# Two layouts of PSUM and the output product among the filler, in a two-layer attention and GLU kernel

## The chip, the cores and the metric

The kernel runs on one core of a Trainium2 chip. The metric is the device time of one execution in microseconds (us). Engines are named as in the profile: PE (matmul), PEld (its weight loads), DVE, ACT, POOL, and SP, whose queue issues most DMAs. PSUM, where PE writes its products, has eight banks of 128 x 512 numbers in fp32 here; DVE and ACT read it.

## The reference

Two layers; each is attention with 16 heads that share one key and one value head, then a gated linear unit. S = 2048 tokens, D = 448, 16 heads of 28, F = 1792.

```python
def _A_ref(x, wq, wk, wv, wo):
    q = (x @ wq).reshape(B, S, H, Dh).transpose(0, 2, 1, 3)
    k = x @ wk
    v = x @ wv
    scores = jnp.einsum("bhqd,bkd->bhqk", q, k) * (Dh ** -0.5)
    o = jnp.einsum("bhqk,bkd->bhqd", _softmax(scores), v)
    return o.transpose(0, 2, 1, 3).reshape(B, S, H * Dh) @ wo
def _B_ref(x, w_gate, w_up, w_down):
    return (_sigmoid(x @ w_gate) * (x @ w_up)) @ w_down
x = x + _A_ref(_layernorm(x), wq, wk, wv, wo)
x = x + _B_ref(_layernorm(x), w_gate, w_up, w_down)
x = x + _A_ref(_layernorm(x), wq, wk, wv, wo)
x = x + _B_ref(_layernorm(x), w_gate, w_up, w_down)
```

## The kernel before

The program is written out instruction by instruction: on each engine, instructions run in the order in which the Python code issues them. What sets that order is a hand-made interleaving of three kinds of work.

**Attention steps.** A layer has 16 query tiles u of 128 rows and, for each, 16 key tiles kt of 128 keys, so 256 steps. One step makes four score tiles s (`scores`, L485, one for each group of four heads; PE product, then an exp on ACT into P, L491), multiplies the four P of the step before with the values into pv (`pv`, L494), and makes the row maxima of four heads of the next query tile against 512 keys (`mx_gen`, L442: four PE products mx into four banks, four reductions on DVE, L462). The string ORDER sets the order within a step: S is one score tile, P is pv, M the maxima, X runs the side work that is due, F hands a slice of time to the filler. Before, it is FSFSFSFSPXM. In query tile 0, two steps (kt 5 and 10, MORE) run M twice. After the 16 groups of one query tile, the maxima are reduced further (m32, m16), transposed on PE (mt), copied (mr) and stored by a DMA from POOL's queue into row 28 of the query tile QS, so that the scores come out with the maximum already taken off.

**Side stages** of a finished query tile (`Block.tile`, L535): sums, reciprocals, oT, the output product wo (`fc`, L584), layer norm, transposition into XT2. Each stage has a delay in steps; `tick` (L514), at X, runs those that are due. `fc` issues its 12 matmuls at once.

**Filler** (`Filler`, L727): generators that issue one matmul at a time, as many as a slice of time pays for: the GLU of a block of two query tiles (`bulk`: gp, up, dn) and the query projections qp of the coming blocks (`qgen`). The rate is the work left over the steps left, until step 48 for the first, and 32 steps for each block. A block's GLU can begin when both of its query tiles are through all side stages, at step 48 at the earliest (`fed`).

In layer 0, `paced` (L269) also runs the preparation of the weights at X: sums of squares on ACT (rmax, L109), then scaling and splitting (sgu, L129, on ACT; L130 on DVE; L140 to L142 on POOL).

Between the layers a loop (L921) ticks, gives four slices of filler each time, and every fifth time (every time for the last four) issues one group of layer 1's maxima for query tile 0, once the keys of those 512 are there (`mx_ready`). The keys come from the GLU's output: dn, layer norm, transposition, kv, transposition into KK.

One PSUM bank is pv's (`psv`). The other seven are one pool, tag f, from which s, mx, qp, gp, up, dn, wo, kv and mt each take a bank that is free:

```python
    NBK = {"f": 7, "s": 2, "m": 3}
    psf = ctx.enter_context(tc.tile_pool(name="psf", bufs=1, space=PSUM))
```

A bank stays taken from the first matmul of a product until its last reader is done; for a product of the filler that is over several steps.

Of the kernel before, what the change touches and what calls it, by code (L numbers as in the profile page):

```python
# [8 lines left out]
F32 = mybir.dt.float32  # L9
# [10 lines left out]
def interleaved_layers_kernel(ctx: ExitStack, tc: tile.TileContext, x, wq, wk, wv, wo, wg, wu, wd, out, layers=2):  # L20
# [23 lines left out]
    BANKS = {"s": "f", "m": "f"}  # L44
    NBK = {"f": 7, "s": 2, "m": 3}
    psf = ctx.enter_context(tc.tile_pool(name="psf", bufs=1, space=PSUM))
# [33 lines left out]
    def fps(shape, dt, name):  # L80
        flush()
        return psf.tile(shape, dt, tag="f", name=name, bufs=NBK["f"])

# [243 lines left out]
    def chain(ps, W, X, cost, w_first):  # L327

        pairs = PAIRS if w_first else sorted(PAIRS, key=lambda a: a[2])
        for n, (part, c, xc, k) in enumerate(pairs):  # L330
            a, b = W(part, c, k), X(xc, k)
            if not w_first:
                a, b = b, a
            nc.tensor.matmul(ps, a, b, start=n == 0, stop=n == 10)  # L334
            yield cost
    sums = [drm.tile([G, 512], F32, name=f"sums{i}") for i in range(2)]
# [34 lines left out]
    def qproj(l, XT, b, g):  # L371
        p = fps([128, 512], F32, "qp")
        yield from chain(p, lambda a, c, k: WQ[:k, a, c, 4 * g:4 * g + 4].rearrange("p h d -> p (h d)"),
                         lambda c, k: XT[:k, c], C512, True)
        by_pool = early[0]
# [21 lines left out]
        defer(ev)  # L397

# [9 lines left out]
    late = []  # L408
    stored = set()
    LT = 1  # L410
# [26 lines left out]
    def mx_ready(l, n):  # L437

        u, r = divmod(n, 4 * NB)
        return KVD[l] >= 4 * (r // 4 + 1) if u == 0 else True  # L440

    def mx_gen(l):  # L442

        load_qh(l, 0)
        for u in range(U):
            qh = QH[l, u]
            mp = wk1.tile([128, 4, 4, NB], F32, name="mp", bufs=2)
            for kb in range(NB):
                for g in range(G):
                    for i in range(len(late) - 1, -1, -1):  # L450
                        late[i][0] -= 1
                        if late[i][0] <= 0:
                            late.pop(i)[1]()
                    assert KVD[l] >= 4 * (kb + 1)
                    ps = [psf.tile([128, 512], F32, tag=BANKS["m"], name="mx", bufs=NBK[BANKS["m"]])
                          for _ in range(4)]
                    for h in range(4):
                        nc.tensor.matmul(ps[h], qh[32 * h:32 * h + 32, g],  # L458
                                         KK[l][32 * h:32 * h + 32, 1, kb * 512:(kb + 1) * 512], start=True,
                                         stop=True, tile_position=(32 * h, 0))  # L460
                    for h in range(4):
                        nc.vector.tensor_reduce(mp[:, g, h, kb:kb + 1], ps[h], axis=AX.X, op=OP.max)  # L462
                    ps = None
                    if kb == NB - 1 and g == 2 and u + 1 < U:
                        load_qh(l, u + 1)
                    if kb * 4 + g == 7:
                        load_qs(l, u)
                    yield
            m32 = wk1.tile([128, 16], F32, name="m32")
            m16 = wk1.tile([128, 16], F16, name="m16")  # L470
            nc.vector.tensor_reduce(m32, mp.rearrange("p g h k -> p (g h) k"), axis=AX.X, op=OP.max)
            nc.vector.tensor_scalar(m16, m32, -(2.0 ** -15), None, op0=OP.mult)

            def fin(u=u, m16=m16):
                stored.add(("m", l, u))
                p = fps([16, 128], F16, "mt")
                nc.tensor.transpose(p, m16, id16)
                r = wk1.tile([16, 128], F16, name="mr")
                nc.vector.tensor_copy(r, p)
                nc.gpsimd.dma_start(QS[l, u][28:29].rearrange("o g h n -> o (g h) n"), r)  # L480
            late.append([LT, fin])
        while late:
            late.pop(0)[1]()
# [468 lines left out]
```

## Time and profile before

| | |
|---|---|
| median of 3 runs | 2375.84 us (2373.78 to 2376.23) |
| span of the profiled execution | 2370.5 us |
| instructions | 40937 |
| first score product of layer 0, of layer 1 | 116.49 us, 1284.04 us |
| last exp of layer 0 | about 1161 us |
| GLU work begins within layer 0, layer 1 | 292.82 us, 1447.92 us |

The page says for each engine how long it was busy. Below, rows of the timeline have the start in us, how long the row lasts, engine, line, operation, output and inputs, how many instructions were merged, and in brackets how long the engine idled before it and what ended the wait. Matmul rows of one kind overlap, so starts, not lengths, give what a matmul costs PE.

### The profile page before, as it was taken

The page shows a single profiled execution, that of the slowest core. Times are in us where ns is not written, and L with a number is a line of the kernel's source. Part 1 is how long each engine was busy: PE and PEld are TensorE (multiplying, and loading weights), DVE is VectorE, ACT ScalarE, POOL GpSimd, SP SyncE. Part 2 cuts the span into 40 slices and gives each one's busy share as a digit, 9 for nine tenths or more (in the row PEclk, how much of TensorE's full clock was granted, in tenths as well). Part 3 has the DMA queues.
Part 4 walks back from the last instruction along what each step waited for, and adds up shares of the span by engine and source line. Part 5 has one row for each costly group of instructions (what it writes and reads, how often), then busy time and mean ns, then how long its engine had stood idle before and what let it go on. Part 6 is the DMA issues. An engine that isn't in the chain of part 4 may idle for free.

```text
span 2370.5 us, 40937 instructions
## 1 busy us (share of the span) xinstructions
PE 2226.5 (94%) x15592; PEld 990.3 (42%) x15592; DVE 1624.5 (69%) x2858; ACT 1560.6 (66%) x2583; POOL 348.7 (15%) x621
## 2 busy tenths in 40 slices
PE   3688899999999999999999989999999999999999
PEld 1221244444444444444573223444444444444456
DVE  3787787777767777774258887777677776777321
ACT  5497767676667767777513777767676776777751
POOL 5403565001111010101011011000000000000010
PEclk9899999999999999999999999999999999999999
DMA  5433563322223132322342112322232222222133
GB/s 145 132 115 95 155 197 111 102 85 71 90 70 108 55 101 85 91 94 63 108 136 57 27 49 82 95 63 87 62 106 63 89 63 91 86 81 93 57 109 120
DMA packets 227525, 218.57 MB, mean 92 GB/s; under 512 B 159408, under 2 KB 187760, under 8 KB 227328
## 3 DMA queue, kind: packets, MB, share of 16 engines
q1 hardware_dynamic: 220832, 200.11, 28.3%
q0 software_dynamic: 5376, 14.87, 1.7%
q8 instruction: 122, 2.00, 0.3%
q10 hardware_dynamic: 1120, 0.98, 0.1%
q14 instruction: 75, 0.61, 0.1%
HBM read 175.37 MB, written 23.59 MB: 84 GB/s over the span
## 4 chain that ended last, share of the span: by engine, by line
PE 78%; DVE 11%; ACT 3%; DMA 2%; issue 2%; SPq 1%; POOL 0%; ACTq 0%; DVEq 0%; POOLq 0%
PE pv L499 19%; PE s L488 16%; PE dn L680 11%; PE gp L334 10%; PE up L334 10%; DVE mp L462 8%; PE mx L458 6%; PE wo L590 3%; ACT P L491 2%; PE qp L334 2%; DVE st L289 0%; DMA qd<-qst 0%; DMA sums<-rc 0%; DMA lb<-sums 0%; DMA XT<-hl 0%
## 5 line engine op out<-in xcount | busy, mean ns | idle before, releaser
L491 ACT ACTIVATE P<-s,esc 128x512 f32<-128x512 f32 x2048 | 1309.2, 690 | 513.2 <-PE s L488 496.1
L462 DVE TENSOR_REDUCE mp<-mx 128x1 f32<-128x512 f32 x2048 | 1268.2, 683 | 408.0 <-PE mx L458 404.1
L488 PE MATMUL s<-QS,KK 96*128 96x512 f16 x2048 | 761.4, 382 | 61.8 <-DVE mp L462 41.1
L334 PEld LDWEIGHTS <-wgu 128*128 128x128 f16 x4928 | 458.1, 97 | 243.5 <-issue 96.8
L499 PE MATMUL pv<-P,VV 128*32 128x512 f32 x4096 | 549.2, 609 | 0.0
L334 PE MATMUL up<-XT,wgu 128*128 128x256 f16 x2464 | 375.6, 272 | 0.0
L334 PE MATMUL gp<-XT,wgu 128*128 128x256 f16 x2464 | 374.2, 273 | 0.2
L680 PE MATMUL dn<-WD,h 128*128 128x448 f16 x1344 | 321.7, 352 | 0.0
L488 PEld LDWEIGHTS <-KK 96*128 96x128 f16 x2048 | 193.1, 97 | 181.3 <-issue 107.9
L458 PE MATMUL mx<-KK,QH 32*128 32x512 f16 x2048 | 217.8, 389 | 17.3 <-DVE mp L462 5.3
L458 PEld LDWEIGHTS <-QH 32*128 32x128 f16 x2048 | 53.6, 91 | 396.8 <-issue 385.6
L680 PEld LDWEIGHTS <-h 128*128 128x128 f16 x1344 | 124.1, 98 | 135.8 <-issue 22.0
L499 PEld LDWEIGHTS pv<-P,VV 128*32 128x32 f32 x4096 | 81.0, 108 | 206.0 <-issue 193.9
L573 POOL TENSOR_TENSOR lb<-pvs,lb 128x512 f32<-128x512 f32 x32 | 40.5, 1265 | 789.0 <-DMA lb<-sums 647.5
L654 ACT ACTIVATE h<-th 128x512 f16<-128x512 f32 x112 | 70.4, 629 | 86.0 <-DVE th L651 85.8
L295 POOL TENSOR_SCALAR rs<-mv 128x1 f32<-128x1 f32 (+2 forms) x53 | 13.4, 252 | 702.4 <-DVE mv L290 691.6
L651 DVE SCALAR_TENSOR_TENSOR th<-th,up 128x512 f32<-128x512 f32 x112 | 76.1, 679 | 56.9 <-PE up L334 44.4
L334 PE MATMUL qp<-XT,WQ 128*128 128x512 f16 x352 | 108.7, 409 | 2.5 <-DVE mp L462 1.2
L655 DVE SCALAR_TENSOR_TENSOR h<-th,h 128x512 f16<-128x512 f32 x112 | 78.8, 703 | 46.1 <-ACT h L654 46.1
L643 ACT ACTIVATE th<-gp,gsc 128x512 f32<-128x512 f32 x112 | 76.9, 687 | 45.8 <-PE gp L334 45.8
L590 PE MATMUL wo<-WO,oT 128*128 128x448 f16 x384 | 78.3, 353 | 0.2 <-DVE oT L580 0.2
L334 PEld LDWEIGHTS <-WQ 128*128 128x128 f16 x352 | 34.0, 102 | 61.3 <-issue 38.8
(117 smaller groups left out, 787.8 us busy)
## 6 DMA issues: line engine op xcount, KB each, us to landing
wgu<-wgu_d SPq DMA_DIRECT2D x224, 512.0 KB
QS<-qd SPq DMA_DIRECT2D x384, 32.0 KB
lb<-sums SPq DMA_DIRECT2D x128, 64.0 KB
xr<-in_A_x_dram SPq DMA_DIRECT2D x32, 224.0 KB
qd<-qst POOLq DMA_DIRECT2D x28, 256.0 KB, 2.6
wgu_d<-sgu POOLq DMA_DIRECT2D x14, 512.0 KB, 3.8
QH<-qd SPq DMA_DIRECT2D x28, 128.0 KB
x2d<-x SPq DMA_DIRECT2D x16, 224.0 KB
```

Source lines behind the costliest of these rows:

```text
L334: nc.tensor.matmul(ps, a, b, start=n == 0, stop=n == 10)
L458: nc.tensor.matmul(ps[h], qh[32 * h:32 * h + 32, g], KK[l][32 * h:32 * h + 32, 1, kb * 512:(kb + 1) * 512], start=True, stop=True, tile_po ...
L462: nc.vector.tensor_reduce(mp[:, g, h, kb:kb + 1], ps[h], axis=AX.X, op=OP.max)
L488: nc.tensor.matmul(s, KK[l][0:96, 0, kt * 128:(kt + 1) * 128], QS[l, u][:, g].rearrange("p h n -> p (h n)"), start=True, stop=True)
L491: nc.scalar.activation(p, s, AF.Exp, scale=esc)
L499: nc.tensor.matmul(v[32 * g:32 * g + 32], VV[l][:, kt], P[g], start=kt == 0, stop=kt == KT - 1, tile_position=(0, 32 * g))
L590: nc.tensor.matmul(p, v["oT"][:, a, h * 128:(h + 1) * 128], WO[:, c, h], start=n == 0, stop=n == 11)
L643: defer(lambda: nc.scalar.activation(th, gp.rearrange("p j n -> p (j n)"), AF.Tanh, scale=gsc))
L651: nc.vector.scalar_tensor_tensor(t, th, 1.0, up.rearrange("p j n -> p (j n)"), op0=OP.add, op1=OP.mult)
L654: nc.scalar.activation(h[:, 0], t, AF.Copy, scale=2.0 ** -17)
L655: defer(lambda: nc.vector.scalar_tensor_tensor(h[:, 1], t, 2.0 ** -17, h[:, 0], op0=OP.mult, op1=OP.subtract), 1)
L680: nc.tensor.matmul(p, hs[f // 2][:, a, o:o + 128], WD[:, f, c], start=n == 0, stop=n == 3 * FC - 1)
```

## The change

There are five parts.

- **PSUM in two layouts.** `layout(kind)` closes one pool and opens another. "even" is the seven banks of before. "split" has three banks with tag f (s, qp, wo, kv, mt and all others) and two tiles of two banks each with tag m for maxima. "split" holds from the program's start, and from each layer's start, until the first block of the layer is fed; then "even". In "split", one DVE reduction takes two heads at once from a tile of two banks.
- **Order within a step.** XSSSFPMFS in "split", XFSFSFSFSPM in "even".
- **wo among the filler.** `fc` only puts a generator on the list `urgent`; each slice issues up to three of its matmuls, ahead of other filler. The stages behind wo are scheduled when it is done.
- **Maxima.** mt follows four slices after the reduction (LAG), by way of `defer`, in place of the next M. mr's DMA is issued from SP's queue in place of POOL's. In layer 1, query tile 0 takes the last 512 keys in two halves, so that the first can run before the last two key tiles are there. The loop between the layers issues a group at every third tick in place of every fifth. QH of the next layer is loaded in the last query tile of the layer before.
- **Query projections of layer 1** for blocks 2 and 3 go to the filler between the layers, in place of layer 1's start.

```diff
-    NBK = {"f": 7, "s": 2, "m": 3}
-    psf = ctx.enter_context(tc.tile_pool(name="psf", bufs=1, space=PSUM))
+    NBK = {"even": 7, "split": 3}
+    def layout(kind):
...
+        banks["scope"] = tc.tile_pool(name=f"psf{banks['n']}", bufs=1, space=PSUM, reuse_waits="tile")
+    def bank(shape, dt, name):
+        return banks["pool"].tile(shape, dt, tag="f", name=name, bufs=NBK[banks["kind"]])
+    def four():
+        if banks["kind"] == "even":
+            ps = [bank([128, 512], F32, "mx") for _ in range(4)]
+            return [(1, p, [p]) for p in ps]
+        ps = [banks["pool"].tile([128, 2, 512], F32, tag="m", name="mx", bufs=2) for _ in range(2)]
+        return [(2, p, [p[:, 0], p[:, 1]]) for p in ps]
...
+    LAG = 4
+    KEYS = {False: [0, 512, 1024, 1536, 2048], True: [0, 512, 1024, 1536, 1792, 2048]}
...
-                    for h in range(4):
-                        nc.vector.tensor_reduce(mp[:, g, h, kb:kb + 1], ps[h], axis=AX.X, op=OP.max)
+                    for n, p, _ in ps:
+                        src = p[:, :k1 - k0] if n == 1 else p[:, :, :k1 - k0]
+                        nc.vector.tensor_reduce(mp[:, g, h:h + n, kb:kb + 1], src, axis=AX.X, op=OP.max)
...
-                nc.gpsimd.dma_start(QS[l, u][28:29].rearrange("o g h n -> o (g h) n"), r)
+            nc.sync.dma_start(QS[l, u][28:29].rearrange("o g h n -> o (g h) n"), r)
...
+            def fc():
+                fill.urgent.append(wo_gen())
...
+            n = 0
+            while self.urgent and n < 3:
+                c = self.next(self.urgent[0])
...
-    ORDER = "FSFSFSFSPXM"
+    ORDERS = {"even": "XFSFSFSFSPM", "split": "XSSSFPMFS"}
...
-        if l:
-            for b in range(2, NB):
-                fill.add(qgen(l, b), G * QCH)
         fill.slice(QCH)
+        layout("split")
...
+            if (l, 0) in BLK and BLK[l, 0].fed == TB:
+                layout("even")
```

What this makes of the order, at three places.

PE in layer 0, query tile 0, before: the four score products of one step with a filler matmul among them, and the start of pv. The names' numbers tell buffers apart; P_1307 to P_1319 are the exps of the step before. In brackets is the engine whose progress the instruction waits for.

```order
L488 MATMUL s_1340<-QS_878,KK_120 128x512 [waits Activation_49]
L334 LDWEIGHTS WQ_89
L334 MATMUL qp_1160<-XT0_127,WQ_89 128x512
L488 LDWEIGHTS KK_120
L488 MATMUL s_1345<-QS_878,KK_120 128x512 [waits DVE_49]
L488 LDWEIGHTS KK_120
L488 MATMUL s_1349<-QS_878,KK_120 128x512 [waits Activation_49]
L488 LDWEIGHTS KK_120
L488 MATMUL s_1353<-QS_878,KK_120 128x512 [waits DVE_49]
L499 MATMUL pv_1213<-P_1307,VV_121 32x512
```

The same place in the change: s_1367 is the last score product of one step, s_1374 to s_1382 are the first three of the next, and P_1344 to P_1369 the exps of the step before.

```order
L531 MATMUL s_1367<-QS_846,KK_120 128x512 [waits Activation_49]
L531 LDWEIGHTS KK_120
L531 MATMUL s_1374<-QS_846,KK_120 128x512 [waits Activation_49]
L531 LDWEIGHTS KK_120
L531 MATMUL s_1378<-QS_846,KK_120 128x512 [waits Activation_49]
L531 LDWEIGHTS KK_120
L531 MATMUL s_1382<-QS_846,KK_120 128x512 [waits Activation_49]
L357 LDWEIGHTS WQ_86
L357 MATMUL qp_1300<-XT0_127,WQ_86 128x512
L542 MATMUL pv_1140<-P_1344,VV_121 32x512
```

Before, the four waited for DVE and ACT in turn, since banks of mx and s mixed; now each waits for ACT alone. s_1374 and s_1382 lie in one bank, s_1367 and s_1378 in another, and qp_1300 is open in the third: s_1382 waits for the exp of s_1374. pv, the next mx and the fourth s stand behind it.

ACT in the same step of the change: P_1369 is the exp of s_1367, P_1376 that of s_1374; rmax is a square of the weights' preparation.

```order
L534 ACTIVATE P_1369<-s_1367,esc_97 128x512 [waits PE_49]
L132 ACTIVATE rmax_1339,mall_791<-rmax_1339 128x784 [waits DMAHW2_49,Activation_49]
L534 ACTIVATE P_1376<-s_1374,esc_97 128x512 [waits PE_49]
L534 ACTIVATE P_1380<-s_1378,esc_97 128x512 [waits PE_49]
L534 ACTIVATE P_1384<-s_1382,esc_97 128x512 [waits PE_49]
L534 ACTIVATE P_1401<-s_1399,esc_97 128x512 [waits PE_49]
```

The square stands between the exp of the last s of a step and that of the first s of the next, as X is now the first letter of a step; before, it stood ahead of the step's four exps as well, but most s waited for DVE or for an exp of the step before.

PE in layer 1, query tile 0, in the change, where no filler is left:

```order
L531 MATMUL s_15451<-QS_14618,KK_1048 128x512 [waits Activation_49]
L531 LDWEIGHTS KK_1048
L531 MATMUL s_15455<-QS_14618,KK_1048 128x512 [waits Activation_49]
L531 LDWEIGHTS KK_1048
L531 MATMUL s_15459<-QS_14618,KK_1048 128x512 [waits Activation_49]
L531 LDWEIGHTS KK_1048
L531 MATMUL s_15463<-QS_14618,KK_1048 128x512 [waits Activation_49]
L542 MATMUL pv_15438<-P_15428,VV_1049 32x512
```

Here all three banks serve s: s_15463, the third of its step, takes the bank of s_15451, the fourth of the step before. Before the change, a step here read as in the first rows, with one or two qp matmuls.

More of the change, by code (lines that the diff above doesn't have):

```diff
@@ L81, in fps @@
         flush()
-        return psf.tile(shape, dt, tag="f", name=name, bufs=NBK["f"])
+        return bank(shape, dt, name)
     C512, C448, C256, C128, C32 = 216, 190, 110, 56, 110
@@ L465, in mx_gen @@
+                    ps = p = src = b = None
+                    if k1 == S and g == 2 and u + 1 < U:
                         load_qh(l, u + 1)
@@ L738, in run, with next, finish @@
         def run(self, gen):
+            cur[0] = None
             for c in gen:
                 self.debt -= c
+        def next(self, gen):
+            cur[0] = gen
+            return next(gen, None)
+        def finish(self):
+            for gen in self.urgent + [g[0] for g in self.gens]:
+                while gen in mid:
+                    self.debt -= self.next(gen) or 0
         def slice(self, ns):
@@ L874, in interleaved_layers_kernel @@
             layer_tiles(l + 1)
-        if l:
-            for b in range(2, NB):
-                fill.add(qgen(l, b), G * QCH)
         fill.slice(QCH)
+        layout("split")
         flush(True)
         next(mx, None)
-        while late:
-            late.pop(0)[1]()
         fill.slice(QCH)
@@ L888, in interleaved_layers_kernel @@
             P = []
+            if (l, 0) in BLK and BLK[l, 0].fed == TB:
+                layout("even")
+            ORDER = ORDERS[banks["kind"]]
             for o in ORDER:
@@ L920, in interleaved_layers_kernel @@
         n = done = 0
-        while (side or pend or fill.gens) if final else (side or pend or done < 4 * NB):
+        last = G * len(parts_of(l + 1, 0))
+        while side or pend or fill.urgent or (fill.gens if final else done < last):
             tick()
```

123 lines of the change are left out of this document (82 added, 41 removed).

## The prediction

> **What bounds the kernel now.** I read first the page's busy lines, then the table by stretches, then, for the stretches where PE idles, the waits of PE and the timeline of single steps. The median of the runs is 2375.84 us; the sum below is made against the profiled execution, whose span is 2370.5 us, so 5.3 us lie around the span.
>
> ```profile
> PE 2226.5 (94%) x15592; PEld 990.3 (42%) x15592; DVE 1624.5 (69%) x2858; ACT 1560.6 (66%) x2583; POOL 348.7 (15%) x621
> 150.00:200.00 50.00, 42.43 (x244) 9.99 (x243) 41.13 (x71) 45.49 (x86) 2.52 (x3) 0.98 0.42 121
> 1300.00:1350.00 50.00, 45.30 (x262) 10.82 (x261) 42.12 (x71) 36.26 (x62) 2.00 (x3) 0.97 0.05 16
> 1500.00:1600.00 100.00, 99.31 (x711) 44.81 (x708) 71.91 (x123) 69.87 (x111) 5.27 (x11) 1.00 0.26 81
> ```
>
> The columns are the stretch in us, its length, busy us of PE, PEld, DVE, ACT and POOL, granted clock, DMA. With GLU work as filler (1500 to 1600) PE has 99% and is the bound: there only added or removed PE work, or new idle, changes the time. In the first 48 steps of each layer (150 to 200, 1300 to 1350) PE has 85 to 91%, and no engine is full. So the change is decided by the step's cycle of waits in those stretches, and by the passage between the layers. One regular step of layer 1, before:
>
> ```profile
> 1293.86 1.07 PE L499 MATMUL pv<-P,VV 128*32 128x512 f32 x8
> 1294.86 0.40 PE L458 MATMUL mx<-KK,QH 32*128 32x512 f16 x4
> 1295.18 0.60 PE L488 MATMUL s<-QS,KK 96*128 96x512 f16 x2
> 1295.28 2.48 DVE L462 TENSOR_REDUCE mp<-mx 128x1 f32<-128x512 f32 x4 [0.58 <-PE mx L458]
> 1295.61 2.42 ACT L491 ACTIVATE P<-s,esc 128x512 f32<-128x512 f32 x4 [0.37 <-PE s L488]
> 1296.62 0.38 PE L488 MATMUL s<-QS,KK 96*128 96x512 f16 x1 [0.22 <-DVE mp L462]
> 1296.93 1.06 PE L499 MATMUL pv<-P,VV 128*32 128x512 f32 x8
> ```
>
> The period is 1296.93 - 1293.86 = 3.07. The last s waits for a bank that DVE frees, pv and the next mx stand behind it, and DVE idles 0.58: a loop of PE and DVE. From these rows: pv to mx 1.00, mx to s 0.32, s to its exp 0.43, last s to pv 0.31. An exp to the s that waits for its bank takes 1379.48 - 1378.74 = 0.74, and exps follow each other at (2.42 - 0.69) / 3 = 0.58:
>
> ```profile
> 1372.43 0.69 ACT L491 ACTIVATE P<-s,esc 128x512 f32<-128x512 f32 x1 [2.63 <-PE s L488]
> 1378.74 2.42 ACT L491 ACTIVATE P<-s,esc 128x512 f32<-128x512 f32 x4 [0.60 <-PE s L488]
> 1379.48 0.82 PE L488 MATMUL s<-QS,KK 96*128 96x512 f16 x2 [0.56 <-ACT P L491]
> ```
>
> **The split layout, a new loop.** Three banks now serve s, qp, wo and mt. By the changed order a step is s1 s2 s3, filler, pv, mx, filler, s4. With all three banks on s, s3 takes the bank of the s4 before it and waits for that exp. pv and mx, ready long before, stand behind s3 on PE, and s4 behind them; ACT runs dry meanwhile. The loop is exp4 to s3 0.74, s3 to pv 0.31, pv to mx 1.00, mx to s4 0.32, s4 to exp4 0.43 to 0.47: **2.81 us**. The DVE loop no longer closes: its four maxima take 2.4, and mx needs only the tile of two heads that was reduced a step earlier.
>
> With a product open in one of the three banks, two are left: s3 waits for exp1 of its own step, which ACT starts 0.58 after exp4: 0.58 + 0.74 + 1.63 + 0.45 = **3.40**. Each filler matmul lies between s3 and s4 and adds its 0.22. Anything that ACT does between exp4 and exp1 adds its full time too. In layer 0 that is a square of the weights (124.61 to 125.45: 0.84) or an sgu copy (237.76 to 238.40: 0.64):
>
> ```profile
> 124.61 0.93 ACT L109 ACTIVATE rmax<-rmax 128x784 f32<-128x784 f32 x1
> 125.45 2.50 ACT L491 ACTIVATE P<-s,esc 128x512 f32<-128x512 f32 x4
> 237.76 0.73 ACT L129 ACTIVATE sgu<-rgu,swb 128x512 f16<-128x512 f32 x1
> 238.40 2.42 ACT L491 ACTIVATE P<-s,esc 128x512 f32<-128x512 f32 x4
> 1301.42 4.88 DVE L462 TENSOR_REDUCE mp<-mx 128x1 f32<-128x512 f32 x8 [0.58 <-PE mx L458]
> 1369.30 2.44 PE L590 MATMUL wo<-WO,oT 128*128 128x448 f16 x12
> 1371.68 0.39 PE L458 MATMUL mx<-KK,QH 32*128 32x512 f16 x4
> 119.79 1.06 PE L499 MATMUL pv<-P,VV 128*32 128x512 f32 x8
> 291.49 1.06 PE L499 MATMUL pv<-P,VV 128*32 128x512 f32 x8
> 1287.72 1.06 PE L499 MATMUL pv<-P,VV 128*32 128x512 f32 x8
> 1446.60 1.07 PE L499 MATMUL pv<-P,VV 128*32 128x512 f32 x8
> ```
>
> Before, such ACT work cost nothing, since ACT had 0.6 free in 3.07 and seven banks let s run ahead; that cover is gone.
>
> **Layer 0.** qp is open in all of steps 1 to 48, as one of its matmuls goes out in two steps of three. So: 48 steps x 3.40 and one x 2.81 = 166; 19 squares x 0.84 = 16; 9 sgu copies x 0.64 = 6; 36 qp matmuls x 0.22 = 8; two steps with double mx, + (4.88 - 2.48) each = 5; 24 wo matmuls x 0.20 (2.38 / 12) = 5; two oT casts and three mt = 2. While wo is open beside qp only one bank is left and each s waits 0.43 + 0.74 = 1.17 for the one before; over four steps that adds 0.9 + 1.8 + 1.8 + 0.8 = 5.3, twice 11. The sum is 219. Before, 47 steps went from 119.79 to 291.49, where GLU work begins: 171.7. After, GLU work begins two steps later, with about 1.75 steps more of attention done, worth 2.3 of PE each (1.00 + 0.32 + 0.97): 219 - 171.7 - 4 = **+43**. Ends: if half of the ACT work falls into other gaps and the single-bank steps cost nothing, +20; if every step also shows 0.2 of DVE or DMA delay, +53.
>
> **Layer 1.** No qp is left, so 49 x 2.81 = 138, double mx 5, wo 5, two-bank steps behind wo 6 x 0.58 = 4, mt and DVE work ahead of a reduction 3, the change of layout about one step of 4, half-clock spells behind the double mx 3: 162, against 1446.60 - 1287.72 = 158.9. Three more steps are then done (7 of PE): **-4**, from -12 to +4. The reduction of two banks at once isn't in the trace: it lies between 0.60 (one bank) and 1.20 (two of them, 2.48 for four). I take near 1.2; it hardly counts, as DVE isn't last in these loops, except for up to 2.4 less in each double step.
>
> **Between the layers.**
>
> ```profile
> 1174.57 0.61 PE L458 MATMUL mx<-KK,QH 32*128 32x512 f16 x4 [3.87 <-DMA QH<-qd]
> 1266.91 0.37 PE L458 MATMUL mx<-KK,QH 32*128 32x512 f16 x1 [0.23 <-DVE mp L462]
> 1269.53 0.74 PE L458 MATMUL mx<-KK,QH 32*128 32x512 f16 x5 [2.25 <-DMA KK<-ktl]
> 1270.50 6.56 PE L458 MATMUL mx<-KK,QH 32*128 32x512 f16 x11 [0.23 <-DVE mp L462]
> 1277.08 4.16 PE L334 MATMUL qp<-XT,WQ 128*128 128x512 f16 x11
> 1281.65 2.55 PE L334 MATMUL qp<-XT,WQ 128*128 128x512 f16 x11
> ```
>
> QH is asked for earlier: -3.9. The last maxima, where PE waited for KK and DVE from 1266.9 to 1277.1, now come in halves of 256 keys among qp matmuls: -10, with 3 for the mx themselves, and -1.8 for the 11 qp at half rate. Against it 66 qp matmuls move here from layer 1's steps: 66 x 0.217 (2.39 / 11) = +14.3; 18 fewer gp and up are left over, -2. The first s now has 1.4 us less behind mt while mr travels through SP's queue, and the new pool waits for the old one: +2. Sum **+2**, from -4 to +6. In POOL's queue the mr transfer no longer stands behind the weight splits; in SP's it is short.
>
> **The GLU stretch.** wo in threes costs PE the same 12 matmuls. But each block is fed some three steps later while the rate still empties the filler at the old step, so 12 steps of the even layout have no filler at all. Such a step took 2.80 before (the page's timeline, 156.34 to 159.14) where PE has 2.3 of work:
>
> ```profile
> 156.34 1.06 PE L499 MATMUL pv<-P,VV 128*32 128x512 f32 x8
> 159.14 1.07 PE L499 MATMUL pv<-P,VV 128*32 128x512 f32 x8
> PE s L488 <- DVE mp L462: 8.9, 25, 0.8
> PE s L488 <- DVE mp L462: 8.1, 24, 0.5
> ```
>
> 12 x 0.5 = +6. The two lower rows are PE's main waits from 450 to 1140 and from 1450 to 2290; a third of their 17 may go with the new order: -6. Taken: **0**, from -11 to +8.
>
> **The clock.** PE runs at half rate behind thin stretches: above, 11 qp took 4.16 at 1277 and 2.55 at 1281. In layer 0 the single-bank steps are as thin: +2, from 0 to +10.
>
> The Trainium skill, "TensorE: Matmul & The Clock Gate", Part 1, states a clock that falls to half after an idle window of about 3.4 us and recovers after a busy one. The trace agrees in kind; no run shows how idle a window must be. By that rule read strictly no step of layer 0 falls, as PE never idles that long, and the sum would be without the 2.
>
> **Sum**: +43 - 4 + 2 + 0 + 2 = +43, span 2413, time 2413.5 + 5.3, about **2418 us**.
>
> **Rivals.** (1) *The loop doesn't bind in layer 0* (0.12): ACT and PE slip past each other so that a step there takes only ACT's own 4 x 0.58 + 0.84 = 3.2. Then 49 x 3.2 + 10 = 167, less 172 and 4: -9, and with -12 and -4 for the rest the time is about 2353. For it: ACT has the capacity. Against it: s3's wait for exp1 is written in the program, and pv stands behind s3. (2) *Balance* (0.07): layer 0 loses only its lower end, 20, and the other terms reach theirs (-12 - 4 - 11): about 2370 to 2380. (3) *Half clock through layer 0* (0.06): with PE busy 2.5 of 4.4 us the clock stays down, the 1.63 from s3 to s4 doubles, 48 x 1.63 = +78: about 2490. For it the row at 1277; against it 0.98 in the first stretch above.
>
> **How the numbers follow.** My forecast has 0.75, its own range is 2394 to 2440. The range below also takes in the balance, and leaves out rivals 1 and 3 (0.18). A measurement of this kernel tells about 0.2% (5 us) from no change. Slower: 0.75 + 0.06 = 0.81; the balance is within 0.2% (0.06) or just faster; faster 0.13.
>
> **What would show it.** Right: from the first s to the first gp in layer 0 about 215 us or more in place of 172; PE's wait for ACT at s in the first 330 us grown from 12 to over 50 us; periods near 4.4 with a square and 3.4 to 3.6 without; 2.8 in layer 1. Wrong: layer 0 steps near 3.1, or DVE named at s again. The passage is right if the 3.87 at the first mx is gone and qp stands among the last mx. If layer 1 stays at 3.07, the three-bank loop is wrong.

## The result, and the profile after

The changed kernel takes 2502.76 us (median of 4 runs, 2499.26 to 2506.59) against 2375.72 before; the ratio is 1.0536, with a 95% interval of 1.0521 to 1.0552. It is 127 us slower. The forecast was 2418, with a range of its own from 2394 to 2440: the right direction, and a third of the size.

From the page of the changed kernel, the busy time of each engine, and the clock granted to PE in 40 equal slices of the span (62.6 us each), in tenths of full speed; the last row is that clock on the page of before:

```profile
PE 2290.2 (91%) x15608; PEld 997.2 (40%) x15608; DVE 1613.6 (64%) x2626; ACT 1577.0 (63%) x2583; POOL 329.7 (13%) x589
PEclk9876789999999999999999999999999999999999
PEclk9899999999999999999999999999999999999999
```

PE is busy 64 us longer with nearly the same instructions, and from the third to the fifth slice the clock is 0.7, 0.6 and 0.7. Before, it was 0.9 there. The loss lies in two places, as the landmarks of the two timelines show (first pv of a layer, first gp after it, last pv of the layer; us):

| stretch | before | after | difference | forecast |
|---|---|---|---|---|
| start to first pv | 119.8 | 119.4 | -0.4 | |
| layer 0, first pv to first gp | 173.0 | 264.5 | **+91.5** | +47 |
| layer 0, first gp to last pv | 866.9 | 889.9 | **+23.0** | -4 |
| between the layers | 128.0 | 133.8 | +5.8 | +2 |
| layer 1, first pv to first gp | 160.2 | 170.1 | +9.9 | +3 |
| layer 1, first gp to last pv | 834.9 | 839.7 | +4.8 | -7 |
| last pv to the end | 87.7 | 85.9 | -1.8 | 0 |

They add up to the 132.8 us between the spans of 2370.5 and 2503.3. The forecast's terms are put here into the stretch in which they fall: its credit for steps that are done by the time GLU work begins (4 in layer 0, 7 in layer 1) belongs to the stretch behind. Its 2 for the clock, also in layer 0, is left out.

The table by stretches has, as before, start and end, length, busy us of PE, PEld, DVE, ACT and POOL, granted clock, and the DMAs. Before, layer 0 up to the first gp:

```profile
119.80:292.80 173.00, 145.79 (x838) 34.68 (x837) 138.30 (x238) 138.87 (x246) 52.85 (x57) 0.95 0.40 117
```

After, the same stretch, and 50 us out of it:

```profile
119.40:383.90 264.50, 199.25 (x859) 39.03 (x859) 138.17 (x145) 147.57 (x250) 55.73 (x58) 0.73 0.28 82
200.00:250.00 50.00, 39.32 (x152) 6.70 (x151) 22.52 (x22) 29.01 (x51) 2.01 (x2) 0.64 0.30 85
```

There are 859 matmuls in place of 838, and 53 us more of busy PE: the matmuls are slower. The start of pv and the start of what follows it show by how much: 1.00 apart in 42 of 48 steps before, but after in only 16 of 49; there it is 1.86 to 1.90 in 22 steps, and in between in 11. One step after, on PE's timeline, and the square on ACT in it:

```profile
176.88 1.94 PE L542 MATMUL pv<-P,VV 128*32 128x512 f32 x8
178.75 0.59 PE L511 MATMUL mx<-KK,QH 32*128 32x512 f16 x4
179.27 0.61 PE L531 MATMUL s<-QS,KK 96*128 96x512 f16 x2
180.44 0.38 PE L531 MATMUL s<-QS,KK 96*128 96x512 f16 x1 [0.56 <-ACT P L534]
181.85 0.38 PE L531 MATMUL s<-QS,KK 96*128 96x512 f16 x1 [1.04 <-ACT P L534]
182.07 0.38 PE L357 MATMUL qp<-XT,WQ 128*128 128x512 f16 x1
182.38 1.77 PE L542 MATMUL pv<-P,VV 128*32 128x512 f32 x8
180.29 0.85 ACT L132 ACTIVATE rmax<-rmax 128x784 f32<-128x784 f32 x1
```

The period is 182.38 - 176.88 = 5.50. The order of waits is the predicted one: after mx the fourth s and the next first s go out, the next two wait for exps, and pv comes last. But pv takes 1.87 from start to start in place of 1.00, and mx 0.52 in place of 0.32. Layer 1, where no product of the filler is open, shows the predicted loop at full clock:

```profile
1411.50 1.06 PE L542 MATMUL pv<-P,VV 128*32 128x512 f32 x8
1412.50 0.40 PE L511 MATMUL mx<-KK,QH 32*128 32x512 f16 x4
1412.83 0.82 PE L531 MATMUL s<-QS,KK 96*128 96x512 f16 x3
1413.99 0.38 PE L531 MATMUL s<-QS,KK 96*128 96x512 f16 x1 [0.34 <-ACT P L534]
1414.30 1.07 PE L542 MATMUL pv<-P,VV 128*32 128x512 f32 x8
```

That is 2.80, where 2.81 was forecast. The view of PE's waits after (total us, times, longest), first two rows over the whole run:

```profile
PE s L531 <- ACT P L534: 82.4, 158, 1.3
PE mt L492 <- DVE m L487: 21.7, 25, 1.2
```

And in layer 0 from the first gp to the last pv, the largest rows before (two) and after (two):

```profile
PE s L488 <- DVE mp L462: 13.8, 35, 0.9
PE mt L477 <- DVE m L472: 2.8, 6, 1.2
```

```profile
PE mx L511 <- ACT P L534: 13.6, 25, 4.8
PE mt L492 <- DVE m L487: 10.7, 12, 1.2
```

The wait for exps at s is the split layout (59.5 of it in layer 0's first stretch). The waits at mt and at mx are in the even layout, and the prediction has neither: PE now waits for DVE at most transposes of the maxima (25 of 32), and for some exps at mx.

### The profile page after: what moved, and what is told of

Read it like the earlier page. It is cut to its first block, busy times and chain, and to the rows that moved or that the text cites. A ratio compares the mean times of both kernels' runs of the same rounds, so it can differ in the third digit from the quotient of the medians.

```text
span 2503.3 us, 40458 instructions
## 1 busy us (share of the span) xinstructions
PE 2290.2 (91%) x15608; PEld 997.2 (40%) x15608; DVE 1613.6 (64%) x2626; ACT 1577.0 (63%) x2583; POOL 329.7 (13%) x589
## 4 chain that ended last, share of the span: by engine, by line
PE 75%; DVE 9%; ACT 6%; DMA 3%; issue 2%; SPq 2%; POOL 1%; ACTq 0%; DVEq 0%; POOLq 0%
PE pv L542 19%; PE s L531 15%; PE gp L357 10%; PE up L357 10%; PE dn L740 9%; DVE mp L517 7%; PE mx L511 6%; ACT P L534 5%; PE wo L634 3%; PE qp L357 2%; DMA wgu<-wgu_d 1%; SPq L459 1%; DMA lb<-sums 1%; ACT rmax L132 1%; SPq L611 0%
## 5 line engine op out<-in xcount | busy, mean ns | idle before, releaser
L534 ACT ACTIVATE P<-s,esc 128x512 f32<-128x512 f32 x2048 | 1326.1, 688 | 570.9 <-PE s L531 546.4
L517 DVE TENSOR_REDUCE mp<-mx 128x1 f32<-128x512 f32 (+2 forms) x1816 | 1255.9, 752 | 567.0 <-PE mx L511 564.9
L531 PE MATMUL s<-QS,KK 96*128 96x512 f16 x2048 | 777.0, 393 | 96.2 <-ACT P L534 82.4
L542 PE MATMUL pv<-P,VV 128*32 128x512 f32 x4096 | 574.7, 634 | 0.0
L357 PE MATMUL up<-XT,wgu 128*128 128x256 f16 x2464 | 370.2, 273 | 2.4 <-DVE mp L517 2.4
L511 PE MATMUL mx<-KK,QH 32*128 32x512 f16 (+1 forms) x2064 | 234.6, 400 | 29.3 <-DVE mp L517 14.7
L713 DVE SCALAR_TENSOR_TENSOR h<-th,h 128x512 f16<-128x512 f32 x112 | 76.9, 687 | 47.7 <-ACT h L712 47.7
L357 PE MATMUL qp<-XT,WQ 128*128 128x512 f16 x352 | 96.9, 404 | 1.7 <-DVE ktl L393 1.7
L634 PE MATMUL wo<-WO,oT 128*128 128x448 f16 x384 | 95.3, 360 | 1.0 <-ACT P L534 1.0
## 6 DMA issues: line engine op xcount, KB each, us to landing
QH<-qd SPq DMA_DIRECT2D x28, 128.0 KB
```

Of the source, the lines that this page charges most:

```text
L511: nc.tensor.matmul(b[:, :k1 - k0], qh[32 * h:32 * h + 32, g], KK[l][32 * h:32 * h + 32, 1, k0:k1], start=True, stop=True, tile_position=(3 ...
L517: nc.vector.tensor_reduce(mp[:, g, h:h + n, kb:kb + 1], src, axis=AX.X, op=OP.max)
L531: nc.tensor.matmul(s, KK[l][0:96, 0, kt * 128:(kt + 1) * 128], QS[l, u][:, g].rearrange("p h n -> p (h n)"), start=True, stop=True)
L534: nc.scalar.activation(p, s, AF.Exp, scale=esc)
L542: nc.tensor.matmul(v[32 * g:32 * g + 32], VV[l][:, kt], P[g], start=kt == 0, stop=kt == KT - 1, tile_position=(0, 32 * g))
L634: nc.tensor.matmul(p, v["oT"][:, a, h * 128:(h + 1) * 128], WO[:, c, h], start=n == 0, stop=n == 11)
```

## The experiments

All are edits of the changed kernel unless it says otherwise. Each ratio is to runs of the kernel before made along with that experiment (medians 2374.16 to 2376.01). Stretches are those of the table above, in us, from the one profiled execution of each, which lies up to 5 us off the median (e2 5.3 above it, e4 5.0 below, e12 4.3 above); GLU means first gp to last pv.

| kernel | median | ratio to before, 95% interval | first stretch 0 | GLU 0 | between | first stretch 1 | GLU 1 |
|---|---|---|---|---|---|---|---|
| before | | | 173.0 | 866.9 | 128.0 | 160.2 | 834.9 |
| after | 2502.76 | 1.0536, 1.0521 to 1.0552 | 264.5 | 889.9 | 133.8 | 170.1 | 839.7 |
| e1 even layout in layer 0 | 2420.45 | 1.0192, 1.0167 to 1.0217 | 187.0 | 890.0 | 130.9 | 165.8 | 838.8 |
| e5 qp of layer 0 first | 2428.24 | 1.0232, 1.0217 to 1.0248 | 191.8 | 881.0 | 132.3 | 167.4 | 839.0 |
| e6 other order in split | 2464.78 | 1.0378, 1.0360 to 1.0397 | 227.7 | 885.4 | 134.6 | 175.5 | 838.8 |
| e2 extra s | 2486.88 | 1.0475, 1.0458 to 1.0491 | 252.4 | 884.7 | 135.7 | 173.0 | 838.8 |
| e11 extra s, not beside wo | 2484.34 | 1.0461, 1.0447 to 1.0474 | 242.5 | 887.6 | 134.3 | 174.1 | 838.7 |
| e3 mt after six slices | 2472.32 | 1.0411, 1.0385 to 1.0438 | 263.7 | 870.8 | 132.1 | 171.6 | 827.4 |
| e4 X behind pv | 2510.72 | 1.0571, 1.0542 to 1.0600 | 263.5 | 889.0 | 131.3 | 169.9 | 842.4 |
| e7 e1, e3 and e4 at once | 2405.24 | 1.0128, 1.0114 to 1.0142 | 175.4 | 887.7 | 131.6 | 170.5 | 830.7 |
| e8 no split, qp back | 2392.74 | 1.0081, 1.0069 to 1.0094 | 177.6 | 886.0 | 128.1 | 161.7 | 832.9 |
| e9 e8 with X in front | 2390.47 | 1.0058, 1.0044 to 1.0073 | 176.8 | 881.6 | 129.9 | 157.3 | 836.7 |
| e10 e8 with mt at the next M | 2368.85 | 0.9975, 0.9964 to 0.9986 | 178.8 | 861.3 | 125.4 | 162.8 | 829.7 |
| e12 e10 with split in layer 1 | 2378.86 | 1.0013, 1.0004 to 1.0023 | 179.6 | 864.6 | 132.5 | 169.6 | 823.9 |

### The first stretch of layer 0

**e1_even0: no split layout in layer 0.**

```diff
-    layout("split")
+    layout("even")
     layer_tiles(0)
...
-        layout("split")
+        layout("split" if l else "even")
```

> Layer 0 keeps seven equal banks and their step order throughout; the split layout is left for the first steps of layer 1. Theory A (two banks for s while qp is open make a step of layer 0 wait, and PE, thinned by that, falls to half clock): first pv to first gp of layer 0 goes from 264.5 back to 170-185 us, granted clock there from 0.73 to 0.95 or more, whole time 2503 - 80 to 95 = 2408 to 2423. Rival B (the loss comes from the work that the change moved, X ahead of the scores, wo in threes, the later mt, whatever the banks): the stretch stays above 220 and the time above 2450.

The time falls by 82 and the stretch to 187.0, 2 above the bound of theory A, with a clock of 0.88 where 0.95 was expected: the split layout of layer 0 makes most of the 91.5. Of the 14 that are left against before, 8 to 12 go with the even layout's waits below, since with those mended as well (e7, e10) the stretch takes 175 to 179.

**e5_qp_first: all three banks for s.** All query products of layer 0 are computed before its first step.

```diff
-        fill.slice(QCH)
+        fill.slice(10 ** 9 if l == 0 else QCH)
         layout("split")
```

> The changed kernel, with all query products of layer 0 computed before its steps, so that no product is open in the split steps and s has all three banks, except while wo is open. Theory A (the open qp leaves two banks, and that makes the step wait): about 28 us of qp move ahead of the steps, and a step falls from 5 to 6 us to 2.8, with a square to 3.6; first pv to first gp from 264.5 to 170-205 us, whole time 2503 - 35 to 65 = 2440 to 2470. Rival E (the order s s s pv mx s, or the weight work on ACT, makes the loop, not the count of banks): the stretch stays above 230 and the time, with the qp in front, is 2495 or more.

Two steps on PE's timeline, the second with a square (ACT, 194.59):

```profile
189.13 1.07 PE L542 MATMUL pv<-P,VV 128*32 128x512 f32 x8
...
191.93 1.06 PE L542 MATMUL pv<-P,VV 128*32 128x512 f32 x8
...
195.07 1.07 PE L542 MATMUL pv<-P,VV 128*32 128x512 f32 x8
194.59 0.88 ACT L132 ACTIVATE rmax<-rmax 128x784 f32<-128x784 f32 x1
```

They take 2.80 and 3.14 in place of 5 to 6; with a square ACT's own work is the bound now (4 x 0.58 + 0.84 = 3.16), less than the 3.6 expected. The stretch falls by 73 and the time by 75, 10 more than expected, though the qp work now stands in front: the first pv comes 10 us later and not 28. The clock is 0.90. With this order of the step, the open qp is what closes the loop.

**e6_order: same banks, pv and mx behind the second s.**

```diff
-    ORDERS = {"even": "XFSFSFSFSPM", "split": "XSSSFPMFS"}
+    ORDERS = {"even": "XFSFSFSFSPM", "split": "XSSPMFSFS"}
```

> The changed kernel, with the split step in the order X s s pv mx filler s filler s: the same banks, but pv and mx stand behind the second score and not behind the third, so they run while s waits for the exps. Theory A (pv and mx held behind s3 close the loop, and ACT's weight work adds to it): a step of layer 0 falls to about 3.4 us with or without a square, the 22 us of squares and copies hide, and PE is fuller, so that some of the half clock goes too: time 2503 - 22 to 50 = 2453 to 2481. In layer 1, with three banks, within 8 us either way. Rival E' (the number of banks alone sets the step): within 10 us of 2503.

Two steps, on PE's timeline, and the square on ACT between their exps:

```profile
122.23 1.07 PE L542 MATMUL pv<-P,VV 128*32 128x512 f32 x8
...
125.61 1.07 PE L542 MATMUL pv<-P,VV 128*32 128x512 f32 x8
...
129.20 1.06 PE L542 MATMUL pv<-P,VV 128*32 128x512 f32 x8
125.14 0.85 ACT L132 ACTIVATE rmax<-rmax 128x784 f32<-128x784 f32 x1
```

They take 3.38 and, with a filler matmul, 3.59; about 3.4 was expected, the squares hidden. That holds for 18 of the 49 steps (3.37 to 3.60); the others are longer, among them those with wo or a second mx, and 13 of the stretch's pv still take 1.87. The stretch falls by 37, its clock rises to 0.84, and the time falls by 38. So it isn't the number of banks alone: with two, it matters whether pv and mx stand behind the s that waits. In layer 1 the first stretch takes 5.4 more (175.5 to 170.1), within the 8 allowed.

**e2_extra_s and e11_extra_s_no_wo: more work for PE.** The score products of the first two groups are computed three times over in the split steps of layer 0; in e11, only while no wo is waiting or open.

```diff
-        nc.tensor.matmul(s, KK[l][0:96, 0, kt * 128:(kt + 1) * 128], QS[l, u][:, g].rearrange("p h n -> p (h n)"),
-                         start=True, stop=True)
+        for _ in range(3 if l == 0 and g < 2 and banks["kind"] == "split" else 1):
+            nc.tensor.matmul(s, KK[l][0:96, 0, kt * 128:(kt + 1) * 128], QS[l, u][:, g].rearrange("p h n -> p (h n)"),
+                             start=True, stop=True)
```

> The changed kernel, but in the split steps of layer 0 the first two score products of each step are each computed three times into their bank: four matmuls more per step, about 200 more, 0.22 us each at full clock, at places where PE otherwise waits. Theory A: the clock falls because PE has too little to do there; with more to do the granted clock of that stretch rises from 0.73 to 0.90 or more, and the time falls by 25 to 45 although work is added (2460 to 2478). Rival C (the waits alone make the loss, or the clock falls for another reason): the clock stays near 0.7 and the time is 0 to 40 longer (2503 to 2545).

> As e2_extra_s, but without the extra score products while wo is waiting or open, where one bank is left and each of them lengthens the step. Theory A (the clock is what the extra work buys, and its price is paid in those few steps): regular steps stay at 4.2 to 4.5 us with a square at full clock, the first stretch of layer 0 falls from 252 to 238-248, and the time from 2487 to 2473-2483. Rival C (the extra work gains in another way): the stretch stays at 252 or more.

One step of e2 on PE's timeline, again with a square:

```profile
157.68 1.06 PE L543 MATMUL pv<-P,VV 128*32 128x512 f32 x8
158.68 0.40 PE L511 MATMUL mx<-KK,QH 32*128 32x512 f16 x4
159.01 0.39 PE L357 MATMUL qp<-XT,WQ 128*128 128x512 f16 x1
159.23 1.97 PE L532 MATMUL s<-QS,KK 96*128 96x512 f16 x7
161.80 0.38 PE L532 MATMUL s<-QS,KK 96*128 96x512 f16 x1 [0.60 <-ACT P L535]
162.11 1.07 PE L543 MATMUL pv<-P,VV 128*32 128x512 f32 x8
```

The period is 4.43, with eight score products in place of four, against 5.50 after without them. It is what the prediction's loop gives for such a step at full clock: 3.40 + 0.84 + 0.22 = 4.46. pv takes 1.00 in 38 of the 49 steps of e2, and in as many of e11. The table by stretches, for e2 and then for e11:

```profile
119.00:371.40 252.40, 209.79 (x1054) 56.55 (x1054) 137.45 (x145) 149.27 (x251) 54.67 (x58) 0.87 0.30 87
```

```profile
120.00:362.50 242.50, 200.41 (x1030) 53.43 (x1030) 138.00 (x145) 149.33 (x251) 54.82 (x58) 0.89 0.30 90
```

With 195 and 171 matmuls more than after, the stretch is 12 and 22 us shorter and the clock 0.87 and 0.89 in place of 0.73. Rival C, 0 to 40 longer at a clock near 0.7, is refuted: work was added and the time fell. The sizes miss on the low side: of the whole time 16 (expected 25 to 45) and 18 us go (20 to 30 by e11's forecast), and the clock stays just below 0.90. e11's stretch is as forecast, but its GLU stretch took 2.9 more than that of e2. What half the clock costs altogether isn't measured by these runs, since the extra products have a price of their own.

### The GLU stretches

**e3_lag6: the transpose of the maxima two slices later.**

```diff
-    LAG = 4
+    LAG = 6
```

> The transpose of a tile's maxima goes out six slices after its reduction, not four. Theory A: in the even layout PE waits for DVE's m at 24 of 32 transposes, 21.7 us in all; two slices later m is ready, and the time falls by 15 to 22 (2481 to 2488), with PE's wait at mt under 5 us. Rival D (PE only trades this wait for the next, DVE's reductions that free the banks): PE's wait at mt goes, but s <- mp grows by as much, and the time stays within 5 of 2503.

PE's wait for DVE at mt is gone from the view, layer 0's GLU stretch falls by 19.1 and layer 1's by 12.3, and the time by 30. Theory A holds in kind, and more was lost than the 21.7 us of the waits themselves: in layer 0's GLU stretch 10.7 of wait at mt go, and with them 4.0 of mx's wait for ACT and 3.9 of PE's busy time, at a clock of 1.00 in place of 0.99. Rival D is refuted: s behind mp waits 8.1 us in all, as after.

**e4_x_last: X behind pv in the even layout.**

```diff
-    ORDERS = {"even": "XFSFSFSFSPM", "split": "XSSSFPMFS"}
+    ORDERS = {"even": "FSFSFSFSPXM", "split": "XSSSFPMFS"}
```

> In the even layout the step's other work (X) stands after pv again, as before the change, and not ahead of the scores. Theory A: at the front, ACT's cast oT follows the queries' 12 transfers on SP's queue by one step less, waits up to 6.3 us for POOL's lb (35.0 us in all) and holds the exps, so that PE's mx waits 13.6 in layer 0; put back, the time falls by 9 to 15 (2488 to 2494), and ACT's wait for lb falls under 8 us. Rival D: ACT has slack enough, PE's wait goes elsewhere, time within 5 of 2503.

Why I expected a gain shows in the changed kernel at 394 to 412 us, on SP's queue (the rows between are weight loads), POOL, ACT and PE:

```profile
394.36 7.81 SPq L459 DMA_DIRECT2D QS<-qd  x12
...
405.71 1.97 SPq L611 DMA_DIRECT2D lb<-sums  x4
```

```profile
409.62 1.25 POOL L616 TENSOR_TENSOR lb<-pvs,lb 128x512 f32<-128x512 f32 x1 [9.57 <-DMA lb<-sums]
```

```profile
410.90 0.62 ACT L622 CAST oT<-lb 128x512 f16<-128x512 f32 x1 [4.64 <-POOL lb L616]
411.43 2.42 ACT L534 ACTIVATE P<-s,esc 128x512 f32<-128x512 f32 x4
```

```profile
412.16 1.74 PE L511 MATMUL mx<-KK,QH 32*128 32x512 f16 x4 [4.76 <-ACT P L534]
```

SP issues lb's four transfers behind twelve for QS, POOL multiplies when they land, ACT waits 4.64 for it with four exps behind, and PE waits 4.76 at mx for a bank that those exps free. Before, X ran a step's length later against QS's transfers. With X put back, mx's wait for ACT in this stretch, 13.6 us, is no longer among PE's waits, as expected, and ACT's for lb falls from 35.0 to 16.4 in all, not under 8. But the time doesn't fall (2510.7 against 2502.8, with intervals that overlap): mt's wait for DVE there grew from 10.7 to 23.5. My price for the single edit was wrong. PE's wait goes elsewhere, as rival D says, though the time isn't within 5 of 2503.

**e7_three_back: even layout in layer 0, six slices, X behind pv.** The diffs of e1, e3 and e4 together.

> Three parts back at once: layer 0 in the even layout, the transpose of the maxima after six slices, and the step's other work behind pv in the even layout. Theory A, if the parts simply add: 2502.8 - 82 (even layout in layer 0) - 30 (six slices) = 2390. Theory F (moving the other work only traded ACT's wait for the cast against a longer wait at the transpose, so with the transpose late it does gain): 10 to 15 less, 2375 to 2380.

2405.24 fits neither. The first stretch is right (175.4), but layer 0's GLU stretch is back at 887.7: with X behind pv, six slices don't help there.

**e8_all_even: no split at all.** e7 with the even layout in layer 1 too, and the query products where they were:

```diff
+        if l:
+            for b in range(2, NB):
+                fill.add(qgen(l, b), G * QCH)
         fill.slice(QCH)
-        layout("split")
+        layout("even")
...
-                        for n in (1, 2):
-                            fill.add(qgen(l + 1, n), G * QCH)
+                        fill.add(qgen(l + 1, 1), G * QCH)
...
-                if u == NT - 1:
-                    fill.add(qgen(l + 1, 3), G * QCH)
```

> The even layout in layer 1 too, and the query products of the later blocks of layer 1 back among its first steps; with the transpose after six slices and the other work behind pv. What is left of the change is the early load of QH, the last maxima in halves, wo in threes among the filler and the later transpose with its transfer on SP's queue. Theory A (these parts cost nothing, and the early QH removes a wait of 3.9 us): 2360 to 2373, faster than before by 3 to 15. Rival G (the passage or wo in threes costs something by itself): 2376 or more.

2392.74, still 18 above the runs of before made with it: theory A fails, and the time lies where rival G put it, but not for G's reason, as e10 shows. Layer 0's GLU stretch (886.0 against 866.9) has all of it. PE's timeline there, and DVE's behind it:

```profile
550.22 1.07 PE L542 MATMUL pv<-P,VV 128*32 128x512 f32 x8
551.22 0.39 PE L511 MATMUL mx<-KK,QH 32*128 32x512 f16 x4
554.64 0.22 PE L492 MATMUL mt<-id,m 128*16 128x128 f16 x1 [3.03 <-DVE m L487]
```

```profile
551.64 2.48 DVE L517 TENSOR_REDUCE mp<-mx 128x1 f32<-128x512 f32 x4 [1.05 <-PE mx L511]
554.16 0.22 DVE L486 TENSOR_REDUCE m<-mp 128x16 f32<-128x64 f32 x1
554.42 0.17 DVE L487 TENSOR_SCALAR m<-m 128x16 f16<-128x16 f32 x1
```

mt stands right behind the mx whose maxima it needs, and waits for all four reductions. Six slices should lie between. The code says why: mt is now in the list of deferred work, and the last part of every dn product (as well as the end of qgen, and `need`) calls `flush(True)`, which issues everything on the list, due or not. Before, mt had a list of its own. Four transposes of layer 0 waited 3.03 each so; the row of dn's last three products stands right behind the mt shown, at 554.80.

**e9_even_x_first and e10_even_late** tell the two causes apart: e9 is e8 with the changed kernel's XFSFSFSFSPM, so that the ends of dn fall on other steps; e10 keeps X behind pv and takes mt out of the list of deferred work:

```diff
-        defer(fin, LAG)
+        late.append(fin)
...
                     assert KVD[l] * 128 >= k1
+                    while late:
+                        late.pop(0)()
                     ps = four()
```

> As e8_all_even, but with the step's other work ahead of the scores, as the change has it. In e8 four transposes of layer 0 waited 3.0 us each for DVE's m, standing right behind the mx whose maxima they need: a product's last part empties the list of deferred work, whatever its lag, and with X behind pv that falls on the wrong step. Theory A: with X in front the lag of six holds, PE's wait at mt in layer 0's GLU stretch goes from 14.7 to under 2 us, and that stretch from 886 to 868-873 us; the time from 2393 to 2373-2380. Rival D (the wait is traded against ACT's wait for the cast, which returns with X in front): 2388 or more.

> As e8_all_even (other work behind pv), but the transpose goes out at the next call for maxima, one step later, as before the change, and no longer through the list of deferred work. Theory A: no transpose is pulled forward any more, PE's wait at mt falls under 5 us, layer 0's GLU stretch from 886 to 866-872 and the time from 2393 to 2370-2378, within 4 of the kernel before. Rival G (wo in threes or the maxima's transfer on SP's queue cost something by themselves): 2383 or more.

Waits of PE in layer 0's GLU stretch: the largest for e9, and then that of mt for e10:

```profile
PE mx L511 <- ACT P L534: 12.7, 20, 5.4
```

```profile
PE mt L493 <- DVE m L488: 2.4, 1, 2.4
```

In e9 mt no longer waits there for DVE, as theory A has it, but ACT's wait for the cast is back, and the stretch takes 881.6 and the time 2390.47, as rival D has it (2388 or more). In e10 both are gone, and the stretch takes 861.3, 25 less than in e8. 2368.85 is below the range of theory A (2370 to 2378), and **faster than before**, by a quarter of a per cent: 0.9975, with an interval from 0.9964 to 0.9986. So wo in threes, the transfer from SP's queue, the halves and the early QH together cost nothing on balance, and rival G is refuted; what each is worth alone wasn't tried. e8 still has one of the two faults and e9 the other, and against e10 they lose 25 and 20 us in this stretch.

### The split layout where s has all three banks

**e12_split_layer1**: e10 with the split layout in layer 1, and layer 1's query products between the layers, as in the change.

```diff
-        layout("even")
+        layout("split" if l else "even")
```

> As e10_even_late, but with the split layout in the first steps of layer 1, and the 66 query products that the change moves there back in the passage: the part of the change in which s has all three banks. Theory A: steps fall from 3.07 to 2.80, 0.27 x 48 = 13, but the query products that before lay beside those steps now cost their 14 us in the passage, and GLU work begins two to three steps later: 0 to 8 longer than e10, 2369 to 2377. Rival H (the three-bank loop pays, since the rest of the step is also ahead): 2366 or less.

2378.86, 10 more than e10 (9 by the ratios) and just above theory A's 0 to 8; rival H is refuted. The passage takes 7.1 more (66 qp more), and the first stretch 6.8 more (with two more steps done in it); the GLU stretch gives 5.8 back. These three make 8 of the 14 by which the two profiled executions differ. A step of 2.80 in place of 3.07 isn't worth the query products that it pushes out.

## Why the prediction was right in direction and wrong in size

The spans differ by 132.8 where the sum has 43. Of the 90 that it missed, 45 lie in layer 0's first stretch, 39 in the two GLU stretches, and the small rest mostly in the passage and layer 1's first steps.

- **The split layout's loops: right.** Three banks give 2.80 (2.81 forecast). Two banks with a square and a filler matmul give 4.43 at full clock in e2 (4.46 forecast). That the open qp and pv behind the third s make the loop is shown by e5 and e6, and that the layout costs layer 0 most of its loss by e1. A reduction of two banks takes 1.22, as taken. Of the signs named, PE's wait for ACT at s in the first 330 us grew to 47.7 (from 13.3, not 12), a little short of the 50; the median step there is 5.5, not 3.4 to 4.4, for the next reason.
- **The clock of layer 0: the step that failed.** The prediction had "+2, from 0 to +10" for it, and gave "half clock through layer 0" a chance of 0.06, with the row of 0.98 (before, 150 to 200 us) against it. That row was of a PE with 85% of work; the loop that I had just derived left it 2.5 of 4.4. The clock was 0.73 in the stretch. Rival 3 counted 78 for a clock that is always half; if it is either full or half, as most pv of the stretch show, at 0.73 it is half for (1 - 0.73) / 0.5 = 54% of the time, and 54% of 78 is 42, where the sum had 2. The stretch exceeds the 219 of the sum by 45. The groups of PE's work in that stretch after (busy us, mean ns, idle before) say the same:

```profile
L542 PE MATMUL pv<-P,VV 128*32 128x512 f32 x392 | 76.8, 867 | 0.0
L511 PE MATMUL mx<-KK,QH 32*128 32x512 f16 x204 | 28.4, 518 | 4.0 <-DVE mp L517 3.9
```

  At full clock 49 times eight pv would be 49 x 1.07 = 52, and 51 times four mx 51 x 0.40 = 20: 33 us more, all of it on the loop. Both 42 and 33 are estimates from rows. That the low clock is a cause and not only a companion is shown by e2 and e11: PE gets more to do, and the stretch becomes shorter.
- **Layer 0's remaining miss** is smaller, and only read off the timeline. The single-bank steps beside wo took more: four steps 25 to 27 us in all where the terms give 21, twice. A second mx in a step waits for the pairs of banks (1.31 and 0.52 us at 172.3 and 173.4), and the two such steps took 7.82 and 8.18, 2.1 and 2.7 more than the step behind each, which is about the 2.4 that was counted.
- **The GLU stretches: "Taken: 0", from -11 to +8, was wrong.** They took 23.0 more in layer 0 and 4.8 in layer 1, although four to five more steps had been done by then (49 and 51 pv in place of 48 and 48; the prediction counted 11 us of PE for them). I went by the steps without filler, and listed the mt that goes out four slices later as part of the change, without asking when its input would be there. DVE takes 2.48 for the four reductions that the transpose needs, behind an mx in the same M, and 0.5 more: four slices of an even step aren't enough. e3 gets 30 us back with one number. The second miss is X ahead of the scores, which moves the cast oT nearer to QS's transfers. e10 has both mended: its GLU stretch of layer 0 is 20 us shorter than that of e9 and 25 shorter than that of e8. So the step that failed here is the same for both: the prediction counted what the new order of the even layout saves, and not the waits that it brings.
- **The passage: +2, from -4 to +6; measured +5.8.** The 3.87 at the first mx is gone, and the qp do stand among the last mx, as said. e8 and e10, without the 66 qp, take 128.1 and 125.4.
- **Layer 1's first steps: about right.** 170.1 us for 51 steps; less two of 2.80, 164.5 for the 49 that were priced at 162.
- **A slip of accounting.** Around the span lie 1.8 us (2505.07 against 2503.3), not the 5.3 taken, which was the distance to another execution's median.

What stays open: how much of layer 0's loss half the clock makes to the microsecond, and why e3, with X in front, keeps layer 0's GLU stretch 11 us shorter than e9. In the traces, 3.1 of it are mx's wait for ACT (9.6 against 12.7), 2.3 a wait of kv for a transfer, and 4.4 busier PE. e3's weight work had 87 us more to get ahead, but no run tried that by itself.

## What to carry to other kernels

When a change lengthens the step on an engine that was nearly full, work out what share of the new step that engine has, and if it falls much, price the loop a second time with the slow clock's durations. Here 2.5 us of work in 4.4 ran at half clock for about half of the time, and the loss in that stretch was 91.5 where the waits alone were priced at 47. A delay counted in slices or steps has to be compared with the time at which its input is ready, and with every place that empties the list it waits in. Mending one fault can make another worse: here X behind pv alone gave nothing, as mt then waited longer. Six slices left 16 us against before with X in front (e9) and 18 with X behind pv (e8), and only X behind pv with mt out of the list made the version that beats both kernels, by 0.25% in the case of the kernel before.

## What was not expected of the hardware

The clock fell although PE never waited long. In layer 0's first stretch after the change, the longest wait of PE is 1.3 us, 93 waits make 59.5 us, and PE is busy for 199 of 264.5 us, most of it with slow matmuls; the clock was 0.64 between 200 and 250 us.

```profile
PE s L531 <- ACT P L534: 59.5, 93, 1.3
```

With three banks, e5's stretch, half of whose steps take 2.80 to 3.15, has 0.90, and the first steps of layer 1 after the change, at 2.80, have 0.83 up to 1450 us and 0.98 and 0.97 in the two stretches of 50 us behind. So short waits were enough for the clock to fall, and what went with it was the share of work in a step; over what time that share counts, no run shows.

The Trainium skill, "TensorE: Matmul & The Clock Gate", Part 1, gives an idle window of about 3.4 us for the fall; read as one gap, the trace speaks against it, with its longest wait of 1.3 us. The same part tells of a kernel that goes round its PSUM banks with short idle spells between groups of matmuls and whose clock swings between half and full; with that, this trace agrees: pv takes 1.86 to 1.90 in 22 of the 49 steps and 1.00 in 16.
